# A layer norm's first blocks: half-block loads on two queues, and ScalarE as a second normaliser, in a fused attention and MLP kernel

## The chip, the core and the metric

The kernel runs on one core of a Trainium2 chip. The core has a matrix engine (TensorE, PE in the profile, with its weight loads as PEld), a vector engine (VectorE, DVE), an activation engine (ScalarE, ACT), a general engine (GpSimd, POOL) and a queue engine that here issues only DMA transfers (SyncE, SP). TensorE writes into PSUM, which has eight banks; the other operands lie in SBUF, and the inputs and outputs in HBM. Each engine works through its own instructions in order and waits on semaphores for the others.

The metric is the device time of one execution in microseconds. The kernel before takes 1569.34 us, the median of three runs that lie between 1569.31 and 1569.5.

## The reference

One input `x` of 2048 tokens by 512 features is layer-normalised. The result goes through two branches, a 32-head attention and an MLP with a tanh-approximated GELU, and the output is gated:

```
xn  = layernorm(x)                                   # 2048 x 512, over the 512
qkv = xn @ wqkv                                      # 512 x 1536
s   = softmax(q k^T / 4, per head of 16) @ v @ wo    # 32 heads
g   = silu(gelu(xn @ w1 + b1) @ w2 + b2)             # hidden size 1376
out = x + s * g
```

Everything is float32. The kernel keeps that precision by splitting each operand into a high part (rounded to the matrix engine's faster float32 form) and a low part (the remainder), and by forming each product from three: high with high, low with high, high with low.

## The kernel before

The tokens are handled as 16 blocks of 128 rows and four chunks of four blocks. A first stage (lines 384 to 525) normalises the blocks, transposes them so that the features lie on the partitions, splits them into `xh` and `xl` (one pair of tiles for each chunk), and makes with them the first Q and K columns (head group 0, lines 445 to 452) and V of blocks 0 and 1 (lines 438 to 443). Behind it a long planned stage mixes the other projections, the MLP and the first attention scores; it is followed by the attention proper and the output projection. In these later stages every instruction's place is written out by a plan made when the kernel is built, and the change leaves the plan as it is.

The order inside each engine's queue is the order of the calls in the source; nothing is rescheduled. In the first stage this order is as follows.

- Loads. `load_x` (line 399) loads a block of 128 by 512 floats, 256 KB, in one transfer; six buffers (`XB`) hold blocks. Blocks 1 and 3 are issued by ScalarE, all others by SyncE. After the first four blocks SyncE issues the two weight blocks of Q and K (line 460), blocks 4 and 5, and four transfers of V's weights `wv_r` (line 464). Block t + 6 is issued when the norm of block t has freed its buffer (line 428).
- Warm-up. TensorE multiplies an identity by itself 22 times into an unused bank (line 482); in the trace these are 44 instructions. Behind them in its queue are the transposes.
- `ln(t, n)` (line 483) is run for a chunk: `moments` for each of its four blocks (two VectorE instructions each), `rstd` for the four together (a chain of six small instructions, of which the square root is ScalarE's and the others VectorE's), then `norm` for each block on VectorE.
- `turn(t)` (line 430): four TensorE transposes of one block into one bank, then `split` (line 74): ScalarE copies the bank into `xh`, rounding it, and VectorE subtracts that from the bank into `xl`.
- `q_first(c)` (line 445): 24 products for two column blocks of a chunk, in the order high-high, low weight, low token. `evac` (line 359) then copies the two banks out by ScalarE, rounds both by ScalarE, subtracts by GpSimd, and issues the stores of the high and low parts to a scratch tensor in HBM (`qk_h`, `qk_l`) on SyncE's queue.
- `v_tile(t)` (line 438): twelve products, the three terms in turn for each of four feature slices.

The order of the calls is: `ln` of chunk 0; the split of the Q/K weights (ScalarE the high parts, GpSimd the low parts, the latter behind `pool_after(3)`, a tiny GpSimd instruction that reads the norm of block 3 and so holds GpSimd until then); the turns of chunk 0; V's high weights by ScalarE and three of its four low weights by GpSimd (`wv_low`); `ln` of chunk 1; constants; the fourth low weight behind the norm of block 7; `q_first(0)`. Then, for each further chunk, come its turns, the `ln` of the next chunk, `v_tile` of the block before, and `q_first`. Since `evac` is called inside `q_first`, ScalarE rounds a chunk's Q and K before it copies the next chunk's transposed blocks.

After `q_first(1)` the kernel calls `load_first` (line 120): twelve transfers on SyncE's queue that read the first keys and queries back from the scratch tensor. The planned stage that starts at line 741 uses them for its first score products (line 190).

Of the kernel before, what the change touches and what calls it, by code (L numbers as in the profile page):

```python
# [8 lines left out]
F32 = mybir.dt.float32  # L9
# [7 lines left out]
P = 128  # L17
# [32 lines left out]
def fused(ctx: ExitStack, tc: tile.TileContext, x, wqk, wv, wo, w1, b1, w2, b2, out):  # L50
# [23 lines left out]
    def split(hi, lo, src):  # L74
        nc.scalar.activation(hi, src, AF.Copy)
        nc.vector.tensor_sub(lo, src, hi.bitcast(F32))  # L76

    def mm3(ps, lhs, rhs, first, last, then=None):
        n = 0
# [204 lines left out]
        nc.sync.dma_start(raw, src)  # L284
        return raw

    def w_split(raw, tag, bufs):
        h, l = [wk.tile([P, CH], F32R, name=tag + x, bufs=bufs) for x in "hl"]
        nc.scalar.activation(h, raw, AF.Copy)
        nc.gpsimd.tensor_sub(l, raw, h.bitcast(F32))  # L290
        return h, l

    ms = [("m", c, f) for c in range(NCH) for f in range(FT)]
    VQ = 3
# [61 lines left out]
    wv_h, wv_l = [kv[:, i].rearrange("p (k d) -> p k d", d=D) for i in range(2)]  # L356
    hl_of = {}

    def evac(us, ph):
        raws = [wk.tile([P, CH], F32, name="hg", bufs=2) for u in us]  # L360
        for u, raw in zip(us, raws):
            if u[0] == "m":
                nc.scalar.activation(raw, ph.pop(u), AF.Gelu_apprx_tanh, bias=b1_sb[:, u[2]:u[2] + 1])
            else:
                nc.scalar.activation(raw, ph.pop(u), AF.Copy)
        for u, raw in zip(us, raws):
            hh = wk.tile([P, CH], F32R, name="hh", bufs=HB)
            hl = wk.tile([P, CH], F32R, name="hl", bufs=HB)
            nc.scalar.activation(hh, raw, AF.Copy)  # L369
            nc.gpsimd.tensor_sub(hl, raw, hh.bitcast(F32))  # L370
            if u[0] == "m":
                HS[u[1:]] = (hh, hl)
            else:
                rs, cs = slice(u[1] * P, (u[1] + 1) * P), slice(u[2] * CH, (u[2] + 1) * CH)
                nc.sync.dma_start(qk_h[rs, cs], hh.bitcast(F32))
                nc.sync.dma_start(qk_l[rs, cs], hl.bitcast(F32))
# [7 lines left out]
    with ExitStack() as s1:  # L384
        wp = s1.enter_context(tc.tile_pool(name="w1p", bufs=1, side="right"))
        w1k = s1.enter_context(tc.tile_pool(name="work1", bufs=2, side="right"))
        banks = [0]

        def a_tile(shape):
            banks[0] += 1  # L390
            i = banks[0] % 6
            if i < 3:
                return (ps_a, ps_b, ps_x)[i].tile(list(shape), F32, name="ps")
            return ps_t.tile(list(shape), F32, name="pst")


        xs, xns = {}, {}

        def load_x(t):
            xs[t] = w1k.tile([P, D], F32, name="xt", bufs=XB)  # L400
            eng = nc.scalar if t in (1, 3) else nc.sync
            eng.dma_start(xs[t], x[t * P:(t + 1) * P, :])
# [4 lines left out]
        ve = wp.tile([P, 5, NT], F32, name="ve")  # L407

        def moments(t):
            st = w1k.tile([P, 6], F32, name="st")  # L410
            nc.vector.bn_stats(st, xs[t])  # L411
            nc.vector.bn_aggr(mv[:, t, :], st)

        def rstd(t0, t1):
            v = ve[:, :, t0:t1]
            nc.vector.tensor_scalar(v[:, 0], mv[:, t0:t1, 1], EPS, None, op0=OP.add)
# [4 lines left out]
            nc.vector.scalar_tensor_tensor(v[:, 4], v[:, 3], 1.5, v[:, 2], op0=OP.add, op1=OP.mult)  # L421

        def norm(t):
            xns[t] = w1k.tile([P, D], F32, name="xn", bufs=4)
            nc.vector.tensor_scalar(xns[t], xs.pop(t), mv[:, t, 0:1], ve[:, 4, t:t + 1],  # L425
                                    op0=OP.subtract, op1=OP.mult)
            if t + XB < NT:
                load_x(t + XB)

        def turn(t):  # L430
            pt = a_tile((P, KT, P))
            xn = xns.pop(t)
            for k in range(KT):
                nc.tensor.transpose(pt[:, k, :], xn[:, k * P:(k + 1) * P], ident)  # L434
            c, ts = t // NCH, slice(t % NCH * P, t % NCH * P + P)
            split(xh[c][:, :, ts], xl[c][:, :, ts], pt)

        def v_tile(t):
            pv = a_tile((P, D))
            c, ts = t // NCH, slice(t % NCH * P, t % NCH * P + P)  # L440
            for k in range(KT):
                mm3(pv, (xh[c][:, k, ts], xl[c][:, k, ts]), (wv_h[:, k], wv_l[:, k]), k == 0, k == KT - 1)
            v_out(t, pv)

        def q_first(c):
            pq = {("q", g, c): a_tile((P, CH)) for g in range(2)}
            for n, (i, j) in enumerate(((0, 0), (1, 0), (0, 1))):
                for g in range(2):
                    for k in range(KT):
                        nc.tensor.matmul(pq["q", g, c], W1[g][i][:, k * P:(k + 1) * P], (xh, xl)[j][c][:, k],  # L450
                                         start=n == 0 and k == 0, stop=n == 2 and k == KT - 1)
# [6 lines left out]
        nc.scalar.activation(warm[:, 1:], warm[:, :1], AF.Sqrt)  # L458
        for g in range(2):
            W1[g] = w_new(wqk[:, g], 2, "raw1")  # L460
        for t in range(4, 6):
            load_x(t)
        for k in range(KT):
            nc.sync.dma_start(wv_r[:, k], wv[:, k])
        for t in range(6, XB):
            load_x(t)
        make_identity(nc, ident)
        nc.gpsimd.memset(vsb[:, :, :H * VW].rearrange("p t (h w) -> p t h w", w=VW)[:, :, :, DH:], 1.0)
        nc.gpsimd.memset(vsb[:, :, H * VW:], 1.0)

        def consts():
            one = w1k.tile([2, 1, P // 2], F32, name="one", bufs=1)
            nc.gpsimd.memset(one, 1.0)
            nc.gpsimd.dma_start(ones_d.rearrange("r (n c) -> r n c", c=P // 2),
                                one.to_broadcast([2, 2 * NT, P // 2]))
            nc.gpsimd.tensor_copy(ident_r, ident)
            nc.gpsimd.dma_start(b1_sb, b1)
            nc.gpsimd.dma_start(b2_sb, b2.rearrange("(o d) -> o d", o=1).to_broadcast([P, D]))

        pw = ps_v.tile([P, D], F32, name="pv")  # L480
        for _ in range(22):
            nc.tensor.matmul(pw[:, :P], ident, ident, start=True, stop=True)
        def ln(t, n):
            for i in range(t, t + n):
                moments(i)
            rstd(t, t + n)
            for i in range(t, t + n):
                norm(i)

        ln(0, NCH)  # L490
        def pool_after(t):
            nc.gpsimd.tensor_sub(warm[:, :1], xns[t][:1, :1], xns[t][:1, :1])

        def wv_low(k):
            nc.gpsimd.tensor_sub(wv_l[:, k], wv_r[:, k], wv_h[:, k].bitcast(F32))

        pool_after(NCH - 1)
        for g in range(2):
            W1[g] = w_split(W1[g], "w1", 4)
        for t in range(NCH):  # L500
            turn(t)
        for k in range(KT):
            nc.scalar.activation(wv_h[:, k], wv_r[:, k], AF.Copy)
# [6 lines left out]
        q_first(0)  # L510
        for c in range(1, NCH):
            for t in range(NCH * c, NCH * c + NCH):
                turn(t)
            if c < NCH - 1:
                ln(NCH * c + NCH, NCH)
            else:
                nc.scalar.activation(warm[:, 1:], warm[:, :1], AF.Gelu_apprx_tanh)
                w1_load(0)
                w2_load(0)
                w2_load(1)  # L520
                break
            v_tile(c - 1)
            q_first(c)
            if c == 1:
                load_first()

    keep_r = ctx.enter_context(tc.tile_pool(name="keep_r", bufs=1, side="right"))
    qring = ctx.enter_context(tc.tile_pool(name="qring", bufs=2, side="right"))
# [525 lines left out]
```

## Time and profile before

| what | value |
|---|---|
| median of three runs | 1569.34 us |
| the profiled execution's own time | 1569.27 us |
| its span in the profile | 1567.4 us |
| granted TensorE clock | 1.00 |
| first score product (line 190) | 44.48 us from the start |

The span is the stretch from the first to the last recorded instruction of the profiled execution; its own time is 1.87 us longer. All stamps below count from the start of the span. The first stage takes the first 41 of the 1567 us. In the timeline, merged rows ("x4") stand for several instructions in a row, and the time is from the first one's start to the last one's end. The name behind a bracket's arrow is what ended the idle time of that engine. `slot` stands for the tiles `xh` and `xl`, `xt` for a loaded block, `xn` for a normalised one, `kt` here for V's weights, `st`, `mv` and `ve` for the statistics and the small steps, `hg`, `hh`, `hl` for Q and K on their way out, `gt` for the first keys and queries.

### The profile page before, as it was taken

To read this page: it belongs to the slowest core of one execution; us is meant where nothing else is said; L and a number is where in the kernel's file an instruction comes from. 1 tells how busy PE (TensorE), PEld (TensorE's weight loads), DVE (VectorE), ACT (ScalarE), POOL (GpSimd) and SP (SyncE) were. 2 spreads that over 40 slices of the span, in tenths; PEclk is the share of its full clock that TensorE was granted. 3 is DMA by queue.
4 is the path that set the end of the run, shared out by engine and by line. 5 is a ranking of instruction groups with operands and counts; after the bars stand their busy time and mean duration, and the time that the engine had idled before them with its cause. 6 is when DMAs were issued, how large, how long until landed. Compare 5 with 4: busy or idle time off the path is not lost.

```text
span 1567.4 us, 32580 instructions
## 1 busy us (share of the span) xinstructions
PE 1556.5 (99%) x12254; PEld 956.3 (61%) x12254; DVE 1390.5 (89%) x2306; ACT 1244.5 (79%) x2487; POOL 375.3 (24%) x392
## 2 busy tenths in 40 slices
PE   9999999999999999999999999999999999999998
PEld 7899999999995444444444444444444444444455
DVE  7899999999998999999999999999999999999733
ACT  4333343434338999999999999999999999999994
POOL 4135574756752000000000100010110000000144
PEclk9999999999999999999999999999999999999999
DMA  7515443355425012311111311141141111110162
GB/s 219 157 47 138 120 153 111 109 150 149 139 89 117 21 42 43 60 30 31 42 29 29 63 31 42 43 73 36 37 74 28 33 29 32 41 30 23 46 214 98
DMA packets 79502, 117.38 MB, mean 75 GB/s; under 512 B 28877, under 2 KB 29133, under 8 KB 77969
## 3 DMA queue, kind: packets, MB, share of 16 engines
q1 hardware_dynamic: 75884, 102.36, 23.8%
q0 software_dynamic: 2976, 12.35, 4.4%
q8 instruction: 97, 1.59, 0.4%
q10 hardware_dynamic: 484, 0.60, 0.1%
q14 instruction: 61, 0.49, 0.1%
HBM read 84.81 MB, written 25.97 MB: 71 GB/s over the span
## 4 chain that ended last, share of the span: by engine, by line
PE 98%; DVE 1%; DMA 0%; issue 0%; ACT 0%; POOL 0%; DVEq 0%
PE pv L801 32%; PE pst L737 15%; PE ps L737 14%; PE ps L569 13%; PE ps L190 10%; PE pst L569 7%; PE pv L569 3%; PE ps L907 1%; PE ps L450 1%; PE ps L81 1%; PE pst L81 1%; DVE st L411 0%; PE pst L434 0%; DMA xt<-in_x 0%; DVE slot L76 0%; DVE xn L425 0%
## 5 line engine op out<-in xcount | busy, mean ns | idle before, releaser
L195 DVE TENSOR_REDUCE mx<-ps 128x2 f32<-128x512 f32 x2048 | 1298.0, 685 | 109.4 <-PE ps L190 32.4
L739 ACT ACTIVATE slot<-pst 128x512 f32<-128x512 f32 x1533 | 803.6, 604 | 2.1 <-PE pst L737 0.8
L801 PE MATMUL pv<-slot,vsb 128*17 128x512 f32 (+1 forms) x4096 | 539.1, 598 | 0.2 <-DVE os L808 0.2
L190 PE MATMUL ps<-kt,slot 48*128 48x512 f32 x1350 | 382.8, 371 | 1.1 <-POOLq L227 1.1
L739 ACT ACTIVATE slot<-ps 128x512 f32<-128x512 f32 x515 | 307.7, 598 | 7.2 <-PE ps L737 4.6
L737 PE MATMUL pst<-qt,kt 50*128 50x512 f32 x1149 | 304.3, 405 | 0.5 <-DVE gt L654 0.3
L737 PEld LDWEIGHTS ps<-qt,kt 50*128 50x128 f32 x387 | 70.6, 183 | 323.8 <-ACT slot L739 322.9
L190 PEld LDWEIGHTS ps<-kt,slot 48*128 48x128 f32 x1350 | 223.2, 184 | 5.7 <-POOLq L227 1.4
L569 PE MATMUL ps<-slot,w1h 64*128 64x512 f32 x1104 | 222.8, 393 | 0.0
L737 PEld LDWEIGHTS pst<-qt,kt 50*128 50x128 f32 x1149 | 207.4, 185 | 22.0 <-DVE gt L654 1.1
L737 PE MATMUL ps<-qt,kt 50*128 50x512 f32 x387 | 190.7, 495 | 0.0
L190 PE MATMUL ps<-kt,qz 48*128 48x512 f32 x448 | 187.0, 418 | 0.0
L190 PE MATMUL ps<-slot,slot 48*128 48x512 f32 x584 | 168.6, 372 | 0.0
L569 PEld LDWEIGHTS ps<-slot,w1h 64*128 64x128 f32 x1104 | 156.1, 185 | 5.0 <-ACT junk L583 0.2
L569 PE MATMUL ps<-slot,w1l 64*128 64x512 f32 x552 | 145.6, 392 | 0.0
L370 POOL TENSOR_TENSOR hl<-hg,hh 128x512 fp32r<-128x512 f32 x76 | 96.8, 1295 | 134.9 <-ACT hh L369 104.9
L801 PEld LDWEIGHTS pv<-slot,vsb 128*17 128x17 f32 (+1 forms) x4096 | 68.8, 96 | 83.4 <-issue 30.5
L583 ACT ACTIVATE junk<-ident_r 1x1 f32<-1x1 f32 x94 | 18.4, 196 | 126.0 <-PE pst L569 117.8
L737 PE MATMUL pst<-qt,slot 50*128 50x512 f32 x384 | 99.7, 404 | 0.0
L190 PEld LDWEIGHTS ps<-slot,slot 48*128 48x128 f32 x584 | 97.0, 184 | 3.1 <-DVE mx L195 0.8
L838 POOL TENSOR_TENSOR slot<-slot,dn 64x512 f32<-64x512 f32 x16 | 20.5, 1282 | 312.4 <-PE pst L737 176.6
L190 PEld LDWEIGHTS ps<-kt,qz 48*128 48x128 f32 x448 | 82.0, 183 | 15.4 <-DVE mx L195 1.0
(153 smaller groups left out, 1767.0 us busy)
## 6 DMA issues: line engine op xcount, KB each, us to landing
raw<-in_w SPq DMA_DIRECT2D x88, 256.0 KB
qk_h<-hh SPq DMA_DIRECT2D x32, 256.0 KB
qk_l<-hl SPq DMA_DIRECT2D x32, 256.0 KB
qt<-qk_h SPq DMA_DIRECT2D x128, 64.0 KB
slot<-qk_h SPq DMA_DIRECT2D x92, 64.0 KB
g_d<-gt POOLq DMA_DIRECT2D x16, 256.0 KB, 3.0
qt<-qk_l SPq DMA_DIRECT2D x64, 64.0 KB
kt<-qk_h POOLq DMA_DIRECT2D x16, 256.0 KB, 5.9
```

Source lines behind the costliest of these rows:

```text
L81: nc.tensor.matmul(ps, lhs[a], rhs[b], start=first and n == 0, stop=last and n == 2)
L190: return nc.tensor.matmul(ps[:, c0:c0 + w], QS[u][r, p, qi * P:(qi + 1) * P], keys, start=True, stop=True).ins
L195: nc.vector.tensor_reduce(MX[u][:, 2 * p:2 * p + 2, qi, ki][:, heads, parts], ps.rearrange("p (n c) -> p n c", c=HC), axis=AX.X, op=OP.max)
L370: nc.gpsimd.tensor_sub(hl, raw, hh.bitcast(F32))
L450: nc.tensor.matmul(pq["q", g, c], W1[g][i][:, k * P:(k + 1) * P], (xh, xl)[j][c][:, k], start=n == 0 and k == 0, stop=n == 2 and k == KT - 1)
L569: i = nc.tensor.matmul(ps, lhs[r], rhs[r], start=first, stop=last).ins
L583: i = nc.scalar.activation(junk[:, :1], ident_r[:1, :1].bitcast(F32), AF.Copy).ins
L737: nc.tensor.matmul(ps, kts[KSET[g]][p][r, k * P:(k + 1) * P], QT[u][r, p, :], start=True, stop=True)
L739: nc.scalar.activation(PT[u, k][:, 2 * p + a, :], ps, AF.Exp, scale=SCALE)
L801: nc.tensor.matmul(PV[u][32 * j:32 * j + w, :], vsb[:, k, h:h + w], PT[u, k][:, j, :], start=(k == 0), stop=(k == NT - 1))
L838: eng.tensor_mul(ot[c][rs, g // 2], ot[c][rs, g // 2], DN.pop(u)[rs])
L907: op = nc.tensor.matmul(PW[b][0], OTS[b, k][i][r], (wo_h, wo_l)[j][r, k], start=part == 0 and n == 0, stop=part == 3 and n == 5).ins
```

## The change

The change touches only the first stage.

- Blocks 0 to 3 are loaded in two transfers of 64 rows each, the upper half by SyncE and the lower half by ScalarE. Later blocks come whole, by SyncE.
- `rstd` has a seventh small step on VectorE (minus the mean times the scale), and `norm` of every odd block is one ScalarE activation with that bias and scale; the even blocks stay on VectorE.
- The high parts of the first Q/K weights are rounded by ScalarE between `rstd` and the norms of chunk 0, and their low parts wait for the norm of block 2 instead of block 3.
- In `turn`, VectorE instead of ScalarE copies the first block of each chunk into `xh`. The other blocks are copied by ScalarE as before, and VectorE still makes all `xl`.
- The statistics of block 7 are made by ScalarE (`act_moments`: two passes with a sum along the row, and one small instruction), the other blocks' by VectorE.
- V's low weights 0 and 1 come before the `ln` of chunk 1, and 2 and 3 behind the norm of block 6. `v_tile` takes its products term by term, with the low weights last.
- The turns of chunk c + 1 are called inside `evac` of chunk c, between the copies from PSUM and the rounding of Q and K.
- `consts` comes after `q_first(0)`.

```diff
         def load_x(t):
             xs[t] = w1k.tile([P, D], F32, name="xt", bufs=XB)
-            eng = nc.scalar if t in (1, 3) else nc.sync
-            eng.dma_start(xs[t], x[t * P:(t + 1) * P, :])
+            if t < NCH:
+                for eng, r0 in ((nc.sync, 0), (nc.scalar, P // 2)):
+                    eng.dma_start(xs[t][r0:r0 + P // 2], x[t * P + r0:t * P + r0 + P // 2, :])
+            else:
+                nc.sync.dma_start(xs[t], x[t * P:(t + 1) * P, :])
...
+        def act_moments(t):
+            sq = xns[t] = w1k.tile([P, D], F32, name="xn", bufs=4)
+            acc = w1k.tile([P, 1], F32, name="acc")
+            nc.scalar.activation(sq, xs[t], AF.Copy, scale=1.0 / D, accum_out=mv[:, t, 0:1])
+            nc.scalar.activation(sq, xs[t], AF.Square, bias=mv[:, t, 0:1], scale=-1.0, accum_out=acc)
+            nc.scalar.activation(mv[:, t, 1:2], acc, AF.Copy, scale=1.0 / D)
...
+            nc.vector.scalar_tensor_tensor(v[:, 5], m[:, :, 0], -1.0, v[:, 4], op0=OP.mult, op1=OP.mult)
...
         def norm(t):
+            if t % 2:
+                nc.scalar.activation(xns[t], xs.pop(t), AF.Identity, bias=ve[:, 5, t:t + 1], scale=ve[:, 4, t:t + 1])
+            else:
+                nc.vector.tensor_scalar(xns[t], xs.pop(t), mv[:, t, 0:1], ve[:, 4, t:t + 1],
+                                        op0=OP.subtract, op1=OP.mult)
...
-            split(xh[c][:, :, ts], xl[c][:, :, ts], pt)
+            if t % NCH:
+                nc.scalar.activation(xh[c][:, :, ts], pt, AF.Copy)
+            else:
+                nc.vector.tensor_copy(xh[c][:, :, ts], pt)
+            nc.vector.tensor_sub(xl[c][:, :, ts], pt, xh[c][:, :, ts].bitcast(F32))
...
+            for n, (i, j) in enumerate(((0, 0), (1, 0), (0, 1))):
+                for k in range(KT):
+                    nc.tensor.matmul(pv, (xh, xl)[i][c][:, k, ts], (wv_h, wv_l)[j][:, k],
+                                     start=n == 0 and k == 0, stop=n == 2 and k == KT - 1)
...
-            evac(list(pq), pq)
+            evac(list(pq), pq, lambda: turns(c + 1))
...
-        ln(0, NCH)
+        for i in range(NCH):
+            moments(i)
+        rstd(0, NCH)
+        high = [w_high(W1[g], "w1", 4) for g in range(2)]
+        for i in range(NCH):
+            norm(i)
...
-        pool_after(NCH - 1)
+        pool_after(NCH - 2)
         for g in range(2):
-            W1[g] = w_split(W1[g], "w1", 4)
+            W1[g] = w_low(W1[g], high[g], "w1", 4)
+        turns(0)
         for k in range(KT):
             nc.scalar.activation(wv_h[:, k], wv_r[:, k], AF.Copy)
-        for k in range(KT - 1):
+        for k in range(2):
             wv_low(k)
-        ln(NCH, NCH)
-        consts()
-        pool_after(2 * NCH - 1)
-        wv_low(KT - 1)
+        act_moments(2 * NCH - 1)
+        ln(NCH, NCH, (2 * NCH - 1,))
+        pool_after(2 * NCH - 2)
+        for k in range(2, KT):
+            wv_low(k)
         q_first(0)
+        consts()
+        for c in range(1, NCH - 1):
+            ln(NCH * c + NCH, NCH)
             v_tile(c - 1)
             q_first(c)
```

More of the change, by code (lines that the diff above doesn't have):

```diff
@@ L357, in fused, with evac @@
     hl_of = {}
-    def evac(us, ph):
+    def evac(us, ph, then=None):
         raws = [wk.tile([P, CH], F32, name="hg", bufs=2) for u in us]
@@ L365, in evac @@
                 nc.scalar.activation(raw, ph.pop(u), AF.Copy)
+        if then:
+            then()
         for u, raw in zip(us, raws):
@@ L406, in fused @@
         mv = wp.tile([P, NT, 2], F32, name="mv")
-        ve = wp.tile([P, 5, NT], F32, name="ve")
+        ve = wp.tile([P, 6, NT], F32, name="ve")
         def moments(t):
@@ L440, in v_tile, with turns @@
             c, ts = t // NCH, slice(t % NCH * P, t % NCH * P + P)
-            for k in range(KT):
-                mm3(pv, (xh[c][:, k, ts], xl[c][:, k, ts]), (wv_h[:, k], wv_l[:, k]), k == 0, k == KT - 1)
+            for n, (i, j) in enumerate(((0, 0), (1, 0), (0, 1))):
+                for k in range(KT):
+                    nc.tensor.matmul(pv, (xh, xl)[i][c][:, k, ts], (wv_h, wv_l)[j][:, k],
+                                     start=n == 0 and k == 0, stop=n == 2 and k == KT - 1)
             v_out(t, pv)
+        def turns(c):
+            for t in range(NCH * c, NCH * c + NCH):
+                turn(t)
         def q_first(c):
@@ L482, in fused, with ln @@
             nc.tensor.matmul(pw[:, :P], ident, ident, start=True, stop=True)
-        def ln(t, n):
+        def ln(t, n, given=()):
             for i in range(t, t + n):
-                moments(i)
+                if i not in given:
+                    moments(i)
             rstd(t, t + n)
@@ L525, in fused @@
                 load_first()
+        nc.scalar.activation(warm[:, 1:], warm[:, :1], AF.Gelu_apprx_tanh)
+        w1_load(0)
+        w2_load(0)
+        w2_load(1)
     keep_r = ctx.enter_context(tc.tile_pool(name="keep_r", bufs=1, side="right"))
```

37 lines of the change are left out of this document (13 added, 24 removed).

## The prediction

> **What bounds the kernel now.** I read the page first: the shares of the engines and the chain that ended last.
>
> ```profile
> span 1567.4 us, 32580 instructions
> ...
> PE 1556.5 (99%) x12254; PEld 956.3 (61%) x12254; DVE 1390.5 (89%) x2306; ACT 1244.5 (79%) x2487; POOL 375.3 (24%) x392
> ...
> PE 98%; DVE 1%; DMA 0%; issue 0%; ACT 0%; POOL 0%; DVEq 0%
> ```
>
> TensorE (PE) is busy for all but 10.9 us of the span, and 98% of the chain is its work. So a change here can give or take only PE's idle time. Next I read the timeline of the head, where the change lies, for those gaps. A row gives the start, the time (of all merged instructions), the instructions, and in brackets the idle time before them with what ended it.
>
> ```profile
> 0.75 0.90 ACTq L402 DMA_DIRECT2D xt<-in_x  x2
> 0.75 0.86 SPq L402 DMA_DIRECT2D xt<-in_x  x2
> ...
> 1.37 7.76 PE L482 MATMUL pv<-ident 128*128 128x128 f32 x44 [1.37 <-POOL ident masks.py:199]
> 1.66 0.91 SPq L284 DMA_DIRECT2D raw<-in_wqk  x2
> 1.68 1.28 ACT L458 ACT_TABLE_LOAD   x1 [1.68 <-PEq L1046]
> ...
> 4.15 2.54 SPq L464 DMA_DIRECT2D wv_r<-in_wv  x4
> 4.15 0.69 DVE L411 BATCH_NORM_STATS2 st<-xt 128x6 f32<-128x512 f32 x1 [3.29 <-DMA xt<-in_x]
> ...
> 7.26 0.18 DVE L412 BATCH_NORM_AGGREGATE mv<-st 128x2 f32<-128x6 f32 x1
> 7.48 0.17 DVE L416 TENSOR_SCALAR ve<-mv 128x4 f32<-128x4 f32 x1
> ...
> 7.80 1.13 ACT L289 ACTIVATE w1h<-raw 128x512 fp32r<-128x512 f32 x2
> ...
> 8.53 0.17 DVE L421 SCALAR_TENSOR_TENSOR ve<-ve 128x4 f32<-128x4 f32 x1
> 8.73 1.92 DVE L425 TENSOR_SCALAR xn<-xt,mv,ve 128x512 f32<-128x512 f32 x4
> ...
> 9.33 1.11 PE L434 MATMUL ps<-ident,xn 128*128 128x128 f32 x8 [0.19 <-DVE xn L425]
> 10.28 1.08 PE L434 MATMUL pst<-ident,xn 128*128 128x128 f32 x8
> 10.65 1.29 DVE L76 TENSOR_TENSOR slot<-ps,slot 128x512 fp32r<-128x512 f32 x2
> ...
> 10.95 2.52 POOL L290 TENSOR_TENSOR w1l<-raw,w1h 128x512 fp32r<-128x512 f32 x2
> 11.00 1.09 ACT L75 ACTIVATE slot<-pst 128x512 fp32r<-128x512 f32 x2
> 11.95 2.21 ACT L503 ACTIVATE kt<-wv_r 128x512 fp32r<-128x512 f32 x4
> ...
> 12.14 1.19 PE L450 MATMUL pst<-slot,w1h 128*128 128x512 f32 x4 [0.78 <-ACT slot L75]
> ...
> 13.06 0.68 DVE L411 BATCH_NORM_STATS2 st<-xt 128x6 f32<-128x512 f32 x1
> ...
> 13.44 3.81 POOL L495 TENSOR_TENSOR kt<-wv_r,kt 128x512 fp32r<-128x512 f32 x3
> ...
> 16.37 0.91 DVE L416 TENSOR_SCALAR ve<-mv 128x4 f32<-128x4 f32 x1
> ...
> 16.91 1.09 PE L450 MATMUL ps<-slot,w1h 128*128 128x512 f32 x4
> ...
> 18.36 2.02 DVE L425 TENSOR_SCALAR xn<-xt,mv,ve 128x512 f32<-128x512 f32 x4
> 18.53 1.15 ACT L369 ACTIVATE hh<-hg 128x512 fp32r<-128x512 f32 x2
> ...
> 19.05 1.09 PE L434 MATMUL ps<-ident,xn 128*128 128x128 f32 x8 [1.05 <-DVE xn L425]
> ...
> 20.91 3.01 PE L81 MATMUL pst<-kt,slot 128*128 128x512 f32 x12
> ```
>
> After the warm-up products (to 9.13) PE has three gaps: 0.19 before the first transposes, 0.78 before the first Q/K products (12.14), 1.05 before the transposes of chunk 1 (19.05). That is 2.02 us in all, the most that shorter waits can give. Behind 19.05 the head's PE rows follow each other with no bracket.
>
> The wait rows explain the gaps. VectorE (DVE) stood idle 3.29 us until the first token block came at 4.15, then took statistics of four blocks to 7.44 (0.82 a block), six small steps to the first norm (7.48 to 8.73, 1.25), and PE began 0.60 behind that norm. For chunk 1 the same chain began at 13.06, and its first small step took 0.91 instead of 0.17: 16.37 + 0.91 = 17.28, just behind GpSimd's (POOL's) three subtractions, which end at 13.44 + 3.81 = 17.25.
>
> **The change, part by part.** All sums stand against the profiled execution (1569.27 us, span 1567.4); the median of the runs, 1569.34, is 0.07 above it.
>
> Loads. Four transfers become eight of half the size, four on each queue. Today two whole blocks share the DMA engines from the start; with halves the first block has both queues. The rate and SP's wait for an earlier transfer:
>
> ```profile
> 2.50:3.00 0.50, 0.50 (x4) 0.50 (x4) 0.00 (x0) 0.49 (x2) 0.00 (x0) 1.00 1.07 385
> 3.00:3.50 0.50, 0.50 (x5) 0.50 (x4) 0.00 (x0) 0.18 (x1) 0.00 (x0) 1.00 1.01 356
> ...
> 36.00:38.00 2.00, 2.00 (x10) 1.64 (x9) 1.62 (x6) 0.30 (x2) 0.00 (x0) 1.00 0.97 120
> ...
> SPq L464 <- DMA xt<-in_x: 1.4, 2, 0.8
> ```
>
> (After the stretch and its length the columns are PE, weight loads, DVE, ACT, POOL, clock, DMA share and GB/s.) The stream runs at about 365 GB/s. No row shows 64-row transfers. One end is that rate kept: block 0 then needs 0.26 MB ahead of it instead of 0.52, which saves 0.72 us, so it lands at 3.43 and the others 0.72 apart, faster than DVE's 0.82. (Today's landing fits: from a start near 2.45, 0.52 MB at 365 end at 3.87, and 0.28 is left to 4.15.) The other end is the nearest slow row, 120 GB/s at a DMA share of 0.97, where gathers and stores mix. I take 365, because these are the same 2 KB rows of the same tensor; the low end is rival 1.
>
> [...]
>
> Issue. The issues cost 0.43 to 0.45 us each, so ACT is busy with them to 2.55 and its table load (1.28) ends at 3.8; the square root needs it at 7. On SP the first W1 load is now the ninth transfer. The wv_r load is the ninth today and waited for block 0 (the wait row), so W1's load now waits to 3.4. Its bytes follow the tokens' directly: 1.57 MB from 2.45 at 365 GB/s end at 6.75, and W1 is rounded from 7.0. Cost nothing; if W1 came after 8.2, ACT's norms of blocks 1 and 3 would slip behind it. wv_r and the later blocks keep their byte order, again nothing.
>
> First chunk. Statistics run from 3.43 to 6.72. The new seventh small step (mean times scale) adds 0.20, so the first norm starts at 6.76 + 1.45 = 8.21, and PE could start at 8.81. But its warm-up lasts to 9.13: start 9.14, gain 0.19. Were block 0 no earlier, the start would be 9.53, a loss of 0.20. Norms 1 and 3 now lie on ACT behind the two W1 roundings (1.13 from 7.0, done by 8.3), at 8.3 and 8.9, ahead of their turns at 9.65 and 10.67. From first transpose to first product took 2.81 (9.33 to 12.14): transposes to 11.36, then ACT's last copy. That path stays, since blocks 1 to 3 are still copied by ACT. Products start at 11.95 and last 5.86 (12.14 to 18.00), to 17.81. Block 0's copy moves to DVE. The nearest row, a PSUM copy of the same size, is
>
> ```profile
> L808 DVE COPY os<-pv x31: 678/681/682, 512.8 to 1499.2; 128x512 f32<-128x512 f32 x31
> ```
>
> at 0.68, and hardly varies. DVE now makes five passes over PSUM from 9.83, each 0.60 by today's pace (10.65 to 13.06 for four), to 12.85. W1's low parts leave POOL at 11.9 (behind norm 2 instead of norm 3), wanted at 13.8.
>
> Second chunk. DVE takes three statistics, 12.85 to 15.3. ACT makes the fourth: its weight copies end 0.19 earlier, at 13.97, then come two 128x512 passes with sums and a small one. The sums have no row. Low end: two passes at 0.57 and 0.2, 1.35. High end: each sum costs another small step, 2.2 with waits. I take 1.8, so 15.8. Seven small steps (1.45) and the 0.65 from norm to transpose put chunk 1's turn at 17.95, behind 17.81: the 1.05 gap shrinks to 0.14, with ends 0 and 0.5. POOL has only two of V's low parts ahead of this (done near 15.1), so no 0.75 is lost at the first step.
>
> [...]
>
> Moved work. V's low parts 2 and 3 start on POOL behind norm 6 (18.4) and end near 21.2; the reordered v_tile wants them at 20.0 + 8 x 0.23 = 21.8 and later: nothing, with 0.6 to spare. The transposes of chunk c+1 already run on PE right behind the products; what changes is ACT's order, copies before the rounding of Q/K. With norms 5 and 7 and two evacuations ahead, xh of chunk 1 is whole at 21.2, wanted at 22.8. Constants go later on POOL, used after 41: nothing. Q/K rounding, though, moves from 18.53 to about 20.8, and its stores with it; that is rival 2.
>
> The sum: -0.19 - 0.91 = -1.1 us, so 1568.2. With the other ends of the unknown steps it is -0.7 to -1.24.
>
> **The rivals.**
>
> Rival 1, halves at a lower rate r, the case on the other side. Every block lands 0.262 MB / r apart from 2.45 on. Half the rate, 183 GB/s, puts block 3 at 2.45 + 5.73 + 0.28 = 8.46, its statistics at 9.3, the transposes at 11.35 and, with chunk 1's chain shifted alike, its turn at 20.25: +1.2, or 1570.5. At 225 GB/s it is nil, at about 138 it passes +3.1, and at the row's 120 GB/s it is +4.0 (1573.3). For it: eight transfers share queues and engines. Against: same rows, same engines, all 16 busy at 365 today. [...]
>
> Rival 2, the first scores wait for their Q and K.
>
> ```profile
> 30.11 1.14 ACT L369 ACTIVATE hh<-hg 128x512 fp32r<-128x512 f32 x2
> ...
> 33.39 0.32 SPq L376 DMA_DIRECT2D qk_l<-hl  x1
> ...
> 38.83 0.30 SPq L142 DMA_DIRECT2D gt<-qk_l  x1
> ...
> 40.57 0.42 SPq L142 DMA_DIRECT2D gt<-qk_h  x1
> ...
> 44.48 0.44 PE L190 MATMUL ps<-gt 48*128 48x512 f32 x1
> ```
>
> Rounding chunk 1's Q/K (30.11) now comes behind ACT's copies of chunk 2: near 31.1. The last store goes to 34.4, and the loads for the first scores, whose issue ran to 40.99, to about 42.0. PE wants them 1.1 earlier than 44.48. The slack shrinks by 2.1 us. The first product reads only the first three of these six loads, issued 1.4 earlier, so they have 2.8 us from issue to use; the other three serve the next product. It decides if a load takes longer than that; block 0, four times the size, took about 3 from issue (0.75 to 1.2) to 4.15, 1.4 of it transfer, so I expect no wait. It could take back 0 to 2.1: 1568.2 to 1570.3.
>
> Rival 3, the square on ACT is not in the table loaded for the square root: two loads at 1.28 on chunk 1's chain, 1570.8. Copy and square root share it today (one load before 40 us); Square itself no row shows.
>
> Rival 4, block 0 lands no earlier though the rate holds: 9.53, then 18.35: 1568.6.
>
> **How the numbers follow.** The forecast, -0.7 to -1.24, gets 0.52, rival 1 0.22 (0.05 of it beyond +3.1), rival 2 0.10, rival 3 0.04, rival 4 0.07, and 0.05 is for a shift that upsets later waits. The range 1567.9 to 1570.4 leaves out rival 1's slow part, rival 3 and the last. A measurement of this kernel tells about 0.2%, or 3.1 us, from no change; PE's gaps total 2.02, so faster by that is nearly excluded: 0.03. Slower by that needs rival 1 under 138 GB/s or an upset later: 0.10. Within: 0.87.
>
> **What would show it.** Right: statistics start near 3.4 with no gap between blocks; transposes at 9.14; the small step after the second statistics at 0.17; chunk 1's transposes near 17.95 with a bracket under 0.5; the first scores near 43.4 with no wait. Wrong: DVE waiting for blocks 1 to 3, a table load between 13 and 18, PE waiting for gt or for V's low part.

## The result: slower by 0.26%

The changed kernel takes 1572.59 us, the median of 22 runs, against 1569.24 us for the kernel before in as many: 3.35 us more. Without one disturbed run of each (4584 and 1580 us) the ratio is 1.0026, with a 95% interval of 1.002 to 1.0031, where the medians alone give 1.0021. The prediction, 1568.2 with a range to 1570.4, had the sign and the size wrong. The other runs also scatter more: from 1571.53 to 1576.44, where the kernel before keeps within about 1 us.

The profiled execution took 1573.86 us, 1.27 above the median; the reason comes below, with the clock. Its page begins with the span, 4.7 us longer than before, while PE's busy time (second line) grew by 2.5.

```profile
span 1572.1 us, 32608 instructions
...
PE 1559.0 (99%) x12254; PEld 957.0 (61%) x12254; DVE 1388.5 (88%) x2304; ACT 1250.1 (80%) x2496; POOL 375.0 (24%) x392
```

The timeline of the head of the changed kernel, in the same columns as before:

```profile
0.75 2.50 SPq L408 DMA_DIRECT2D xt<-in_x  x4
0.75 2.80 ACTq L408 DMA_DIRECT2D xt<-in_x  x4
...
1.38 6.79 PE L512 MATMUL pv<-ident 128*128 128x128 f32 x44 [1.38 <-POOL ident masks.py:199]
...
3.94 0.69 DVE L419 BATCH_NORM_STATS2 st<-xt 128x6 f32<-128x512 f32 x1 [3.07 <-DMA xt<-in_x]
...
5.47 0.69 DVE L419 BATCH_NORM_STATS2 st<-xt 128x6 f32<-128x512 f32 x1 [0.62 <-DMA xt<-in_x]
...
7.43 0.69 DVE L419 BATCH_NORM_STATS2 st<-xt 128x6 f32<-128x512 f32 x1 [0.15 <-DMA xt<-in_x]
...
10.29 1.09 PE L454 MATMUL ps<-ident,xn 128*128 128x128 f32 x8 [2.12 <-DVE xn L445]
11.22 1.53 PE L454 MATMUL pst<-ident,xn 128*128 128x128 f32 x8
13.43 2.07 PE L480 MATMUL pst<-slot,w1h 128*128 128x512 f32 x4 [0.69 <-ACT slot L457]
...
15.54 0.63 ACT L425 ACTIVATE xn<-xt 128x512 f32<-128x512 f32 x1
...
16.08 0.18 ACT L425 ACTIVATION_READ_ACCUMULATOR xn<-xt 128x1 f32 x1
...
17.01 1.75 PE L480 MATMUL pst<-slot,w1l 128*128 128x512 f32 x4
...
17.38 0.17 DVE L431 TENSOR_SCALAR ve<-mv 128x4 f32<-128x4 f32 x1 [0.78 <-ACT mv L427]
...
21.40 1.04 PE L454 MATMUL ps<-ident,xn 128*128 128x128 f32 x8
```

Three things stand in it. The blocks come late: block 0 lands at 3.94 (4.15 before, 3.43 expected), but block 1 only at 5.47 and block 3 at 7.43, with VectorE waiting for them three times, so the first transposes begin at 10.29 instead of 9.33. TensorE's warm-up, on the other hand, was done at 8.17 and not at 9.13, so TensorE stood idle for 2.12 us instead of 0.19. And from there on its products are slow: four of 128x512 take 2.07 or 1.75 us where they took 1.09 to 1.19. The next view, stretches of 1 us, says why. Its last columns are the granted clock, the DMA share and GB/s. The first two lines are of the kernel before, the others of the changed kernel.

```profile
3.00:4.00 1.00, 1.00 (x7) 1.00 (x6) 0.00 (x0) 0.18 (x1) 0.00 (x0) 1.00 1.00 356
4.00:5.00 1.00, 1.00 (x7) 1.00 (x7) 0.81 (x3) 0.00 (x0) 0.00 (x0) 1.00 1.00 367
...
3.00:4.00 1.00, 1.00 (x7) 1.00 (x6) 0.06 (x1) 0.42 (x1) 0.00 (x0) 1.00 0.82 232
4.00:5.00 1.00, 1.00 (x8) 1.00 (x8) 0.81 (x2) 0.99 (x2) 0.00 (x0) 1.00 0.86 266
...
11.00:12.00 1.00, 1.00 (x10) 1.00 (x9) 0.96 (x2) 0.91 (x3) 1.00 (x2) 0.81 1.06 404
12.00:13.00 1.00, 0.75 (x4) 0.34 (x2) 1.00 (x3) 0.74 (x3) 1.00 (x2) 0.50 1.09 348
...
17.00:18.00 1.00, 1.00 (x4) 0.79 (x3) 0.35 (x2) 0.52 (x4) 0.00 (x0) 0.50 0.00 0
18.00:19.00 1.00, 1.00 (x5) 0.81 (x4) 0.86 (x6) 0.13 (x1) 0.00 (x0) 0.78 0.00 0
```

The granted clock is 0.81 at 11 to 12, 0.50 to 18 and 0.78 in the stretch behind it, where it was 1.00 throughout. And the loads ran at 232 and 266 GB/s where whole blocks had 356 and 367.

The wait before chunk 1's transposes is gone: their row at 21.40 has no bracket. At the end of the first stage the planned stage starts at 43.42 instead of 41.36, 2.06 late. That is less than half of the 4.7. The rest is lost by two waits in the planned stage, which the kernel before does not have; the first view below lists who waited for whom on TensorE from 43 to 130 us, the second follows the chain that ended last, from 44 to 62 us (start, time, what).

```profile
PE ps L186 <- DMA kt<-qk_l: 1.0, 1, 1.0
PE ps L186 <- issue: 0.5, 1, 0.5
```

```profile
43.65 0.42 SPq L138
...
44.12 1.56 SPq L138
...
46.19 0.42 SPq L138
...
47.64 5.54 DMA qk_h<-hh
...
53.20 6.88 DMA kt<-qk_l
...
60.43 0.47 PE ps L186
```

Read from the end: a score product at 60.43 waits for keys (`kt`), whose load was issued at 53.20 and took 6.88; that load waited for a store of the third chunk's Q and K, issued at 47.64, which took 5.54; and the store had stood on SyncE's queue behind the loads of the first queries (L138), the last of which was issued at 46.19.

Brackets show only waits that leave an engine empty, so I measured what the waits cost by marks that exist in every kernel: the start of the planned stage, and the evacuations of its first and second group of V blocks. From the first mark to the second is 9.99 us before and 11.24 now (+1.25); from the second to the third 13.74 and 15.48 (+1.74). So the profiled execution loses 2.06 + 1.25 + 1.74 = 5.05 us by 70 us, and 4.6 of it is left at the end.

### The profile page after: what moved, and what is told of

The parts are those of the page before. It is cut to its first block, busy times and chain, and to the rows that moved or that the text cites. A ratio compares the mean times of both kernels' runs of the same rounds, so it can differ in the third digit from the quotient of the medians.

```text
span 1572.1 us, 32608 instructions
## 1 busy us (share of the span) xinstructions
PE 1559.0 (99%) x12254; PEld 957.0 (61%) x12254; DVE 1388.5 (88%) x2304; ACT 1250.1 (80%) x2496; POOL 375.0 (24%) x392
## 4 chain that ended last, share of the span: by engine, by line
PE 96%; DMA 2%; DVE 1%; ACT 0%; SPq 0%; issue 0%; POOL 0%; ACTq 0%; DVEq 0%
PE pv L834 32%; PE pst L770 15%; PE ps L770 14%; PE ps L602 13%; PE ps L186 10%; PE pst L602 7%; PE pv L602 2%; PE ps L940 1%; PE ps L77 1%; DMA kt<-qk_l 0%; PE pst L77 0%; DMA qk_l<-hl 0%; DMA qk_h<-hh 0%; PE pst L480 0%; DMA xt<-in_x 0%
## 5 line engine op out<-in xcount | busy, mean ns | idle before, releaser
L616 ACT ACTIVATE junk<-ident_r 1x1 f32<-1x1 f32 x94 | 18.4, 196 | 126.1 <-PE pst L602 116.9
```

The source lines that it names most:

```text
L616: i = nc.scalar.activation(junk[:, :1], ident_r[:1, :1].bitcast(F32), AF.Copy).ins
```

## The experiments

Two theories stood at the start. One: three separate costs, the late blocks, the halved clock behind the idle stretch, and the late keys and queries, the last because ScalarE now rounds Q and K behind the copies of the next chunk. Its rival: one cost, the late blocks, from which the rest follows. The table has the marks of each kernel's profiled execution and the median of its runs; the kernel before had medians of 1569.24 to 1569.32 beside them. Each experiment has eleven runs, and its interval reaches about 1.4 us to either side, so smaller differences between medians are not shown by the medians alone. The versions e5 to e8 ran on another chip than the other experiments.

| kernel | planned stage starts | to first V group | to second | median |
|---|---|---|---|---|
| before | 41.36 | 9.99 | 13.74 | 1569.24 |
| changed | 43.42 | 11.24 | 15.48 | 1572.59 |
| e1_whole_loads | 40.40 | 11.50 | 15.66 | 1571.63 |
| e2_more_warm | 42.12 | 11.35 | 15.76 | 1572.72 |
| e3_round_first | 43.79 | 10.75 | 13.81 | 1571.94 |
| e4_halves_alone | 42.52 | 9.96 | 13.75 | 1569.80 |
| e5_first_early | 40.22 | 9.91 | 15.98 | 1571.58 |
| e6_early_and_round | 40.16 | 10.48 | 13.88 | 1568.90 |
| e7_few_warm | 43.75 | 10.01 | 13.76 | 1570.15 |
| e8_halves_no_waits | 41.30 | 10.47 | 13.91 | 1569.64 |
| e9_column_halves | 41.63 | 9.97 | 13.74 | 1568.87 |
| e10_columns_no_waits | 41.09 | 10.44 | 13.77 | 1568.67 |
| e11_round_only | 40.13 | 11.58 | 15.71 | 1571.77 |

### Whole blocks in the changed kernel (e1_whole_loads)

```diff
-            if t < NCH:
-                for eng, r0 in ((nc.sync, 0), (nc.scalar, P // 2)):
-                    eng.dma_start(xs[t][r0:r0 + P // 2], x[t * P + r0:t * P + r0 + P // 2, :])
-            else:
-                nc.sync.dma_start(xs[t], x[t * P:(t + 1) * P, :])
+            eng = nc.scalar if t in (1, 3) else nc.sync
+            eng.dma_start(xs[t], x[t * P:(t + 1) * P, :])
```

> The changed kernel, but blocks 0 to 3 are loaded whole, as before. Theory 'late blocks and cold clock': the halves brought block 3 at 7.43 us instead of about 6.1, the transposes began at 10.29 instead of 9.33, and the 2.12 us in which TensorE stood idle behind its warm-up halved its clock from 11.8 to 18.5. With whole blocks the transposes start near 9.5, the clock stays at 1.00, and the planned stage starts near 40.6 instead of 43.42; the waits of the first scores (about 3 us between 46 and 62) stay, so about 1571.3. Rival 'the halves did not matter, ScalarE's extra work at the start did': transposes still behind 10, no change beyond 0.5 us.

The transposes began at 9.65, the clock stayed at 1.00 in the profiled execution, and the planned stage started at 40.40, 0.96 earlier than in the kernel before. So the rest of the first stage's change does what the prediction's sum said of it: chunk 1's transposes came at 18.35 instead of 19.05, with no wait, although the first ones came 0.32 later. But both later waits stayed (+1.51 and +1.92), and the time is 1571.63, ratio 1.0015 (1.0006 to 1.0024). So 2.35 of the 3.35 us are still there: most of the loss is not in the loads. The rival of one cost falls here.

### More warm-up (e2_more_warm)

```diff
-        for _ in range(22):
+        for _ in range(33):
```

> The changed kernel with 33 warm-up products instead of 22, so that TensorE has work until about 10.1 us. Nothing else is touched, the blocks land as late as in the changed kernel. Theory 'cold clock': the clock stays at 1.00 from 11 to 19, the first Q/K products take 5.9 us instead of 8.1, the planned stage starts near 41.1 (43.42 in the changed kernel's profile), and the runs above 1573.5 are gone: median near 1571.9. Rival 'the late blocks alone cost the 2 us': no change in the start of the planned stage and in the spread of the runs.

With no idle stretch the clock was 1.00 throughout, and the planned stage started 1.30 earlier than in the changed kernel's profile (42.12 against 43.42). The median, 1572.72, did not fall: the 33 products lasted to 11.76 in the profiled execution, past the 10.29 at which the transposes could have begun, so it seems that the longer warm-up took what the clock gave. The runs still scatter (1570.9 to 1574.57), which this theory had not expected; the three slowest have a mean granted clock of 0.998, so in some executions it seems to fall without an idle head, though no trace here shows where (more on this in the last section).

### Rounding before the copies again (e3_round_first)

```diff
-            evac(list(pq), pq, lambda: turns(c + 1))
+            evac(list(pq), pq)
+            turns(c + 1)
```

> The changed kernel, but ScalarE rounds a chunk's Q and K before it copies the next chunk's transposed blocks, as before (the turns are called behind the evacuation). Theory 'late keys and queries': the rounding moved behind the copies pushed the stores and so the loads of the first keys and queries, and TensorE waited for them near 47 to 49 and near 58 to 60; the lag between the start of the planned stage and 68 us, 3.0 us now, falls below 0.5, and the median falls by 2.5 to 3, to about 1569.8. Rival 'the stores are late since the blocks and the cold clock are late': the lag stays at 3 us, no change.

The second wait is gone (13.81). Of the first, 0.76 us are left (10.75), but no score waits for a load any more: the first one now waits for VectorE's last subtraction in the first stage (0.38). The median fell only by 0.65, to 1571.94, and not by the 2.5 to 3 expected. The transposes of chunks 1, 2 and 3 now wait for their norms, 0.87, 0.27 and 0.27 us, and the planned stage starts at 43.79. The order that holds back the scores is the one that keeps the first stage short: each order costs something.

### Half blocks alone (e4_halves_alone)

The kernel before, with the half-block lines of the changed `load_x`.

> The kernel before, with the half-block loads alone. Theory 'halves slow the first blocks': statistics of block 3 end near 8.3 instead of 7.44, transposes begin near 10.1, TensorE idles about 1 to 2 us behind its warm-up, and the time rises by 0.7 us, with some runs 2 to 3 us higher by a halved clock; no waits of the first scores. Rival 'halves bring block 0 earlier and cost nothing': no change within 0.3 us.

```profile
0.75 2.52 SPq L403 DMA_DIRECT2D xt<-in_x  x4
0.75 2.81 ACTq L403 DMA_DIRECT2D xt<-in_x  x4
...
4.11 0.69 DVE L414 BATCH_NORM_STATS2 st<-xt 128x6 f32<-128x512 f32 x1 [3.24 <-DMA xt<-in_x]
...
5.77 0.69 DVE L414 BATCH_NORM_STATS2 st<-xt 128x6 f32<-128x512 f32 x1 [0.75 <-DMA xt<-in_x]
```

The blocks land as late as in the changed kernel, in the timeline's rows above, and the transposes begin at 10.51. The planned stage is 1.16 late, but of that only 0.52 us is left in the median (1569.80 against 1569.28; ratio 1.0004, 0.9995 to 1.0013). No score waits. The clock stayed at 1.00 in this profile, with 1.04 us of idle time; two of the eleven runs have a mean of 0.997, at 1570.88 and 1571.36.

### Early loads of the first keys and queries (e5_first_early), and one chunk's rounding too (e6_early_and_round)

Both have whole blocks. The first edit moves the twelve loads ahead of the second chunk's products; the second version has the other edit besides.

```diff
             v_tile(c - 1)
-            q_first(c)
             if c == 1:
                 load_first()
+            q_first(c)
...
-            evac(list(pq), pq, lambda: turns(c + 1))
+            if c < 2:
+                evac(list(pq), pq, lambda: turns(c + 1))
+            else:
+                evac(list(pq), pq)
+                turns(c + 1)
```

> The changed kernel with whole blocks (as in the first experiment), and the twelve loads of the first keys and queries are called before the second chunk's Q and K products instead of behind them, so that on SyncE's queue they no longer stand behind that chunk's stores. Theory 'the first scores wait because their loads stand behind stores that the new rounding order made late': the 0.9 us wait near 45 goes, the later wait near 58 (for the other keys) stays at about 1.9, time 1570.7. Rival 'the transfers themselves are slower now': both waits stay, 1571.6.

> As the one before, and in the third chunk ScalarE rounds Q and K before it copies the last chunk's transposed blocks, as in the kernel before; its stores come earlier by some 1.5 us, and the loads of the other keys behind them. Theory 'late keys': the second wait goes too; the planned stage starts near 40.4 and the lead of 1 us lasts, 1568.3, faster than before. Rival 'copies later hold up the products that follow': the planned stage loses what the waits give, 1569 to 1570.

The early loads took the first wait away entirely (9.91), and the median did not move: 1571.58 against 1571.63. The second wait grew to 2.24 (15.98), and the clock seems to have taken the rest: seven of the eleven runs have a mean granted clock of 0.997 or 0.998 (1571.18 to 1572.63), where e1_whole_loads has three (1573.1 to 1573.5). The other runs lie at 1569.69 to 1570.77 here and at 1569.93 to 1571.95 there. With both edits the second went too (13.88), and the median is 1568.90. It is above the 1568.3 expected: the later copies do hold something up, in part as the rival said. The first score product waits for VectorE's last subtraction (L457), and 0.49 us of lag is back at the first mark (10.48).

```profile
43.72 0.50 PE L186 MATMUL ps<-gt 48*128 48x512 f32 x1 [0.29 <-DVE slot L457]
```

The ratio of this version to the kernel before, 0.9997, has an interval of 0.9988 to 1.0006 and so does not tell the two apart; against the changed kernel it is 3.7 us less, and its slowest run (1569.46) lies below the fastest of e1_whole_loads (1569.93) and e5_first_early (1569.69).

### The second edit without the first (e11_round_only)

> The changed kernel with whole blocks and the third chunk's old rounding order; the loads of the first keys and queries stay behind the second chunk's stores. Theory 'the wait that ends last is that for the other keys, and taking away the first alone only lengthened it': with the second cause gone, what is left is the first wait of about 0.9 to 1.5, so 1569.8, against 1571.6 with both causes and 1571.6 with the second alone. Rival 'only both together help': 1571.3 or more.

Here the rival won: 1571.77, both waits in place (11.58, 15.71). The reason is SyncE's queue, where the loads of the first queries stand ahead of the third chunk's stores and those ahead of the loads of the other keys. In the row of the profiled execution below, two of the query loads take 1.83 to issue (0.89 in the kernel before; the trace does not show why), and the store of the third chunk comes behind them at 43.82 although its rounding was done at 41.2.

```profile
40.95 1.83 SPq L138 DMA_DIRECT2D gt<-qk_h  x2
...
43.82 0.37 SPq L380 DMA_DIRECT2D qk_h<-hh  x1
```

So the second wait has two sufficient causes: the stores are held by the late rounding, or by the query loads ahead of them. Taking away one leaves the other.

### The same two edits with half blocks (e8_halves_no_waits)

> The changed kernel with its half-block loads kept, but with the early loads of the first keys and queries and the third chunk's rounding order of the two experiments above. Theory 'three separate costs' (late blocks and idle clock about 2, first keys 1.3, other keys 1.7): only the first is left, the planned stage starts at 41.5 to 43.5 and no score waits; 1569.3 to 1571.5. Rival 'the score waits come from the late blocks': they stay, 1572.5.

1569.64: the waits are worth 2.95 us of the changed kernel's 1572.59, and the two intervals lie apart. What the half blocks cost on top of the version with whole blocks is 0.74, and what the rest of the change gives there is 0.42; both are within the intervals.

### Less warm-up in the kernel before (e7_few_warm)

```diff
-        for _ in range(22):
+        for _ in range(13):
```

> The kernel before with 13 warm-up products instead of 22; nothing else is changed. TensorE then stands idle from about 6.7 to 9.33, some 2.6 us, as it did for 2.12 in the changed kernel. Theory 'the idle time behind the warm-up halves the clock': the granted clock falls to 0.50 for several us behind 10 us, the first products take up to 8 us instead of 5.9, and the time rises by 1 to 3 us with a scatter of a few us. Rival 'the low clock in the changed kernel came from something else': clock 1.00 as before, time within 0.3 us of before.

```profile
9.59 1.97 PE L434 MATMUL ps<-ident,xn 128*128 128x128 f32 x8 [3.48 <-DVE xn L425]
```

```profile
8.00:9.00 1.00, 0.00 (x0) 0.00 (x0) 0.67 (x5) 1.00 (x3) 0.00 (x0) 0.56 1.07 399
...
17.00:18.00 1.00, 1.00 (x4) 0.71 (x4) 0.93 (x4) 0.00 (x0) 1.00 (x2) 0.50 0.00 0
18.00:19.00 1.00, 1.00 (x5) 0.82 (x4) 0.69 (x3) 0.21 (x1) 0.68 (x3) 0.82 0.00 0
```

The first row is of the timeline: TensorE stood idle for 3.48 us in the profiled execution, ahead of the first transposes. The others are stretches of 1 us of the same kernel, with the clock third from the end: it is down to 0.56 in the stretch at 8, 0.50 from 9 to 18, and 0.82 behind that. With nothing else changed, the planned stage started at 43.75, 2.39 late. That shows the low clock behind an idle stretch without the rest of the change. Over the runs the median rose by only 0.83 us, with single runs from 1569.05 to 1572.69: the same shorter warm-up does not cost the same in each execution.

### Halves by columns (e9_column_halves, e10_columns_no_waits)

```diff
-            eng = nc.scalar if t in (1, 3) else nc.sync
-            eng.dma_start(xs[t], x[t * P:(t + 1) * P, :])
+            if t < NCH:
+                for eng, c0 in ((nc.sync, 0), (nc.scalar, D // 2)):
+                    eng.dma_start(xs[t][:, c0:c0 + D // 2], x[t * P:(t + 1) * P, c0:c0 + D // 2])
+            else:
+                nc.sync.dma_start(xs[t], x[t * P:(t + 1) * P, :])
```

> The kernel before, with blocks 0 to 3 in two transfers on the two queues, each of all 128 rows and half the columns, instead of half the rows. Theory 'a 64-row transfer moves slower': with all rows in each transfer the rate is that of whole blocks, block 0 lands near 3.5 and the statistics of block 3 start near 6.0 (5.8 to 6.6 in the kernel before, 7.72 with row halves), and the time is at or below that of before. Rival 'eight transfers on two queues are slow whatever their shape': statistics start at 4.0, 5.8, 6.7, 7.7 as with row halves, time 0.5 us above before.

> The version with whole blocks, early loads of the first keys and queries and the third chunk's old rounding order, but with the column halves in place of whole blocks. If column halves land early, the transposes start near 9.2 and the time is some 0.4 us below that version's 1568.9; if they are as slow as row halves, the planned stage starts near 41.3 and the time is about 1569.6.

```profile
0.75 1.81 SPq L403 DMA_DIRECT2D xt<-in_x  x4
...
0.75 1.86 ACTq L403 DMA_DIRECT2D xt<-in_x  x4
...
3.65 0.69 DVE L414 BATCH_NORM_STATS2 st<-xt 128x6 f32<-128x512 f32 x1 [2.78 <-DMA xt<-in_x]
...
6.03 0.69 DVE L414 BATCH_NORM_STATS2 st<-xt 128x6 f32<-128x512 f32 x1 [0.67 <-DMA xt<-in_x]
```

The same count of transfers, queues and bytes, but all 128 rows in each: four issues take 1.81 to 1.86 us, not 2.5 to 2.8, block 0 lands at 3.65 (4.11 with half the rows in the same kernel), and the statistics of block 2 start at 6.03 (6.66) and those of block 3 at 6.86 (7.72, and 6.57 with whole blocks). Most of the loss was in the 64-row shape. The kernel before with column halves takes 1568.87 against 1569.30 beside it (ratio 0.9997, 0.9989 to 1.0006), and the version without waits 1568.67 (0.9995, 0.9986 to 1.0004). The last is the fastest median of all, 0.63 us under the kernel before; its interval still holds 1, so that it beats that kernel is not shown, while it is 3.9 us under the changed one. Its head does not explain the lead: in its profile the transposes start at 9.38, as expected, but those of block 1 wait 0.91 us for ScalarE's norm, and the planned stage starts at 41.09, 0.93 later than with whole blocks.

## Why the prediction was wrong

The step that decides the sign is the one under "Moved work": the waits that it held for nothing are worth 2.95 of the 3.35 us. The loads cost the expected gain.

**Loads.** The step "One end is that rate kept" and its choice, "I take 365", failed. The rate was 232 to 266, and the blocks landed 1.16 us apart, not 0.72. By the prediction's own formula that is 225 GB/s, where rival 1 is nil, and puts the transposes at 10.26; they came at 10.29. So rival 1 priced the slow loads well: they take the gain and not much more. "The issues cost 0.43 to 0.45 us each" failed as well: four take 2.50 and 2.80. The column halves, with all 128 rows in each transfer, show that most of the loss is in the 64-row shape (statistics of block 3 at 6.86, against 7.72). No row of the kernel before showed that shape, and I put the weight on the likeness of the rows.

**First chunk.** "But its warm-up lasts to 9.13" took one execution's row for a property. The same 22 products ended at 8.17 in the changed kernel, and between 7.92 and 9.47 in the other profiles that have 22. So TensorE was free a microsecond earlier than the step had it; the late blocks made the transposes come 1.15 later, and the gap between the two was 2.12. This is chance in part: e8_halves_no_waits, with the same code up to there, has 9.30, a gap of 1.33 and a clock of 1.00. What differs is when the warm-up speeds up. In the changed kernel TensorE does 8 of its instructions in the stretch from 4 to 5 and 12 in the next; in the kernel before it does 8 from 6 to 7 and 12 from 7 to 8. The clock column reads 1.00 in all of these, so it does not show this slower start.

**The clock.** No step and no rival of mine had it. Behind the idle 2.12 us the clock was at half from about 11.6 to 18.4 (worked out from the means of 0.81 and 0.78 in the first and the last of those stretches), and the products 13.43 to 21.57 took 8.14 us instead of 5.86: +2.3 in the profiled execution, the largest term of the head. Of the runs (without that of 4584 us), the 13 with a mean granted clock of 0.999 or more lie between 1571.53 and 1573.5, the 8 below it between 1573.86 and 1576.44. The median run, then, has little of this cost; the scatter is mostly this. How long an idle stretch has to be for this is not shown: the clock fell behind 2.12 us here and 3.48 in e7_few_warm, and did not behind 1.80 (e3) and 1.67 (e6) in the executions profiled.

**Second chunk.** Right. ScalarE's statistics took 15.54 to 17.35, 1.81 with two small instructions of 0.18 that read the sums, against the 1.8 taken; the first small step took 0.17, with GpSimd idle from 16.51 on, where in the kernel before it took 0.91 and ended 0.03 behind GpSimd's subtractions (that these lengthened it is an inference from the two stamps); the 1.05 gap went to nothing. No table load came between 13 and 18, so rival 3 is out. In the changed kernel the slow products would have covered a gap of this size in any case; e1_whole_loads, at full clock, is the clean case: from the first transposes to chunk 1's it takes 8.70 us instead of 9.72, 1.02 less where the sum had 0.91.

**Moved work.** The sentence "so I expect no wait" failed. Rival 2, the wait of the first scores for their queries and keys, was given 0.10 and 0 to 2.1 us; it came, and with 1.25 it lies within its price. Beside it stands a wait of 1.74 for the other keys, which no step and no rival had, beyond the 0.05 "for a shift that upsets later waits". Together they are 3.0, the main cause of the median's rise. The lateness was in part as worked out: the roundings of chunk 1 came 2.2 us later than before against the start of the planned stage (34.36 against 43.42, and 30.11 against 41.36), where the step had 2.1. But in e1_whole_loads, with the clock at 1.00, the last of the six query loads was issued by 43.89 and not by about 42.0, since the roundings came 1.6 later instead of 1.0 (31.72) and one pair of loads took 1.77 to issue instead of 0.89. What I left out is the queue behind it: in the trace the query loads wait for the second chunk's stores (1.6 and 0.5 us; 1.6 and 0.3 in the kernel before), the next chunk's stores stand behind the query loads, and the loads of the other keys, needed at 55.87 in the kernel before, wait for those stores. I followed the moved rounding to its first reader and stopped there.

**The sum.** "PE's gaps total 2.02, so faster by that is nearly excluded" held. The chance of slower by over 0.2%, 0.10, went to a slow transfer rate or an unnamed upset; the rise came from rival 2, the wait for the other keys behind it and, in some runs, the clock.

## What to carry to other kernels

Follow a moved step past its first reader: along the issuing queue, ask what stands behind each transfer that it delays, and whether the work that is moved earlier on one engine makes the reader wait sooner for what it moved later. Where a wait has two causes in a row, undoing one of them may change nothing (1571.6 to 1571.8 in three versions here), so test the pair. And a stretch in which TensorE waits may cost more than its length: behind 2.12 us of it the products ran at a clock of 0.50 and took 8.14 us instead of 5.86. A warm-up should last until the real work comes, but its end moved from one execution to the next (7.92 to 9.47 with the same 22 products), and one that lasted longer than needed, to 11.76, gave nothing here (e2_more_warm).

## What the runs showed of the hardware

Two transfers on two queues over 64 rows each were slower than two over 128 rows with the same bytes: 0.62 to 0.70 us to issue one against 0.45 to 0.47, block 0 at 3.94 to 4.11 against 3.55 to 3.65, and the statistics of block 3 from 7.38 to 7.78 against 6.53 to 6.86. The granted clock fell to 0.50 behind idle stretches of 2.12 and 3.48 us and took until about 18.4 to come back, some 8 us from the first transposes at 10.29. The fall did not always come while TensorE was idle: in the changed kernel it came at about 11.6, 1.3 us after the transposes had begun, and in e7_few_warm at about 8.1, 2.0 us into the idle stretch. Part of a lag went away later. With half blocks alone the 1.16 us at the start of the planned stage are still 1.14 at the second V group; near 478 us, where ScalarE's first work of the attention proper starts (478.18 against 477.44), 0.74 are left, and 0.52 in the median. The lead of 1.20 in e6_early_and_round shrinks early: 0.63 of it is lost by the second V group, by the table, and 0.42 is left in the median.

A lower mean clock went together with the waits in the planned stage. In the three kernels with whole blocks that keep at least one of them (e1_whole_loads, e5_first_early, e11_round_only), 12 of 33 runs have a mean granted clock of 0.997 or 0.998; in the three with whole or column blocks and no wait for queries or keys (e6_early_and_round, e9_column_halves, e10_columns_no_waits), none of 33 is below 0.999. On each of the two chips taken alone it is the same: 5 of 22 against none of 22, and 7 of 11 against none of 11. But none of the profiled executions fell on such a run in the first three, so where in them the clock drops is not shown.
